# A second Strassen level in four products of a down projection, on one core

## The chip, the core and the metric

The kernel runs on one core of a Trainium2 chip. Its engines are called PE (TensorE: matmuls; PEld: its weight loads), DVE (VectorE), ACT (ScalarE), POOL (GpSimd) and SP (SyncE, which here issues every DMA). A matmul multiplies a stationary 128x128 tile (`lhsT`) with a moving one of up to 512 columns (`rhs`) and adds into PSUM, eight banks of 512 float32 per partition. The metric is the device time of one execution in microseconds; the median of three is given.

## The reference

A pre-norm transformer block over 2048 tokens of width 1024: linear attention, then a gated feed-forward of inner width 3584.

```python
x = A_x
h = x + _A_ref(_layernorm(x), A_wqkv, A_wo)          # linear attention, 32 heads
...
gate = jnp.einsum("bsd,df->bsf", x, W_gate)           # x is here _layernorm(h)
up = jnp.einsum("bsd,df->bsf", x, W_up)
gate = gate * (gate > 0)
h = gate * up
return jnp.einsum("bsf,fd->bsd", h, W_down)           # the down projection
...
h2 = h + _B_ref(_layernorm(h), B_W_gate, B_W_up, B_W_down)
```

## The kernel before

Every large product is done in Strassen's form as Winograd wrote it. A (tokens by inner width) and B are cut in 2 x 2 blocks, and seven products of block sums take the place of eight of blocks. With S1 = A21 + A22, S2 = S1 - A11, S3 = A11 - A21, S4 = A12 - S2 on the left and T1 = B12 - B11, T2 = B22 - T1, T3 = B22 - B12, T4 = B21 - T2 on the right, the products are, numbered as in the code: 1 = A11 B11, 2 = A12 B21, 3 = S4 B22, 4 = A22 T4, 5 = S1 T1, 6 = S2 T2, 7 = S3 T3. Then C11 = 1 + 2, U2 = 1 + 6, U3 = U2 + 7, C12 = U2 + 5 + 3, C21 = U3 + 4, C22 = U3 + 5. Block sums are float16, blocks bfloat16.

**Stages.** Layernorm with the K and V products, Q with attention, the output projection with the second layernorm, the *up stage* (gate and up), the *down stage*. Two halves s = 0, 1 of 512 tokens per block row run through the later stages.

**Up stage.** A loop over `order` runs 28 quads (s, fc): one per half and per block of 128 inner columns (14, fc). A `Quad` is the seven products of one output set in the order 1, 6, 5, 7, 2, 4, 3 on three accumulators: product 1 goes into bank A, and ACT copies it to D (`fork`); 6 is added in A and read out as U2 (`snap`); 5 goes into E; 7 is added in A and read as U3; 2 into D, 4 into A, 3 into E. `Quads.run` moves a quad's last two products behind the next quad's first, so that readers have time. A product is here 8 matmuls of 512 columns. ACT takes the snapshots (`gsnap`), DVE adds, applies the gate and writes the four results `hh` (a11, a12, a21, a22 of the down projection's left side). For s = 0 they stay in memory (`hh0`, 84 KB to 140 KB of each partition), for s = 1 `spill` stores them in `hh_dram`. Gate and up weights come in groups of two blocks (`load_group`), and DVE makes their four right sums (`GW.sums`).

**Down stage.** `down(s)` runs for s = 0 and then 1. Each of the seven products is four token tiles (`tt`) of 14 matmuls of 512 columns, 3 us per tile, and four A banks and four E banks hold a whole product each. DVE makes four left sums of 14 x 512 per half (`sA`, `sB`, `s3`, `s4`) and, for s = 0 only, four right sums `t1` to `t4`, each in two pieces of 7 x 512 (3584 elements), during the products. It adds the residual h, which is loaded again from `h_dram`, and stores the output through the two buffers of `o2_ring`. W_down comes in four loads of 1.8 MB, the first in the up stage; for s = 1 four loads of 1.8 MB bring `hh_dram` back.

```python
        def f6(tt):
            prod(A[tt], tt, sB, t2, False)
            u2[tt] = plus_h(A[tt], 1, tt)
```

**What sets the order.** The whole program is recorded by `Plan.take` as nodes with predecessors; all of them are recorded at line 117, which is why every row of the profile has that line. `order` gives each node a latest start (`late`); `schedule` then simulates the engines with the costs of `cost`, lets each take the ready node with the smallest `late` (TensorE: the smallest place in the program, no more than 6 us of work ahead), counts all DMAs on one serial `wire`, and `issue` writes the instructions out in that order. On the chip each engine runs its own list in order.

Of the kernel before, what the change touches and what calls it, by code (L numbers as in the profile page):

```python
# [9 lines left out]
ALU = mybir.AluOpType  # L10
FP32 = mybir.dt.float32
# [21 lines left out]
class Plan:  # L33
# [75 lines left out]
    def take(self, eng, op, args, k):  # L109
# [31 lines left out]
        for a in outs:  # L141
            name, gs = self.granules(a)
            last, readers = self.state.setdefault(name, ({}, {}))
            for q in gs:
                w = last.get(q)
                if w is not None:
                    v.preds.add(w)
                r = readers.pop(q, None)
                if r:
                    v.preds |= r  # L150
                last[q] = me
# [29 lines left out]
    def schedule(self):  # L181
# [11 lines left out]
        while True:  # L193
# [36 lines left out]
            if v.dma:  # L230
                wire = max(wire, s + v.hold) + v.dma
                end = wire + v.lat - v.dma
# [218 lines left out]
def block_kernel(ctx: ExitStack, tc: tile.TileContext, x, wqkv, wo, wg, wu, wd, out, H: int):  # L451
    nc = tc.nc
# [29 lines left out]
    h_dram = [dram.tile([P, D], BF16, name=f"h_dram{t}") for t in range(ST)]  # L482
    hh_dram = [dram.tile([P, FH, SW], BF16, name=f"hh_dram{q}") for q in range(4)]
# [463 lines left out]
    class Tile_:  # L947
# [54 lines left out]
        def square(self):  # L1002
            h = self.h
            nc.sync.dma_start(out=h_dram[self.t][:], in_=h)
            self.negm = negm = scratch("negm2", 1)
            nc.vector.tensor_scalar(out=negm[:], in0=self.acc[:, 0:1], scalar1=self.acc[:, 1:2], scalar2=-1.0 / D,
                                    op0=ALU.add, op1=ALU.mult)
            self.hn = hn_ring()
            self.ss = scratch("ss", 1)
            tick.late.append(self.square2)  # L1010
# [60 lines left out]
    T_A = (72, 156, 188, 196)  # L1071
    hh1_ring = ring_of([at(180 + i, [SW]) for i in range(8)])

    def hh0(q, fc):
        return at(84 + 4 * fc + q, [SW])

    def gu_quad(s, fc, gw, banks):
# [8 lines left out]
        def dst(q):  # L1086
            return hh0(q, fc) if s == 0 else hh1_ring()

        def spill(q, d):
            if s != 0:  # L1090
                nc.sync.dma_start(out=hh_dram[q][:, fc, :], in_=d)
# [5 lines left out]
        def direct(q):  # L1097
            def f(ps):
# [4 lines left out]
                spill(q, d)  # L1103
# [3 lines left out]
        def added(q):  # L1107
            def f(ps, u):
# [5 lines left out]
                spill(q, d)  # L1114
# [43 lines left out]
    order += [(s, fc) for fc in range(4, FH) for s in range(NS)]  # L1158
    todo = deque([(1, 1, 72), (2, 2, 156), (3, 3, 72), (6, 0, 188), (7, 1, 196)])
    todo.extend((2 * fc, fc, T_A[(fc + 2) % 4]) for fc in range(4, FH))  # L1160
# [12 lines left out]
    b11, b21, b12, b22 = (at(a, [FH, DW]) for a in (164, 0, 14, 28))  # L1173
    t1, t2, t4 = (at(a, [FH, DW], FP16) for a in (42, 56, 178))
    t3 = b12.bitcast(FP16)
    sA, sB = (at(a, [FH, SW], FP16) for a in (70, 150))
    hres_ring = ring_of([at(192 + i, [DW]) for i in range(8)])
    m2_ring = ring_of([at(140 + 2 * i, [DW], FP32) for i in range(4)])
    m3_ring = ring_of([at(a, [DW], FP32) for a in (148, 202)])
    o2_ring = ring_of([at(200 + i, [DW]) for i in range(2)])  # L1180

    def load_wd(b, k, h):
        nc.sync.dma_start(out=b, in_=wd_v[:, k * FH:(k + 1) * FH, h * DW:(h + 1) * DW])

    quads = qs
    for n, (s, fc) in enumerate(order):
# [12 lines left out]
        if n in loads:  # L1199
            load_group(loads[n])  # L1200
        elif n == 24:
            load_wd(b11, 0, 0)
# [5 lines left out]
    load_wd(b21, 1, 0)  # L1208
    load_wd(b12, 0, 1)
    load_wd(b22, 1, 1)  # L1210

    hq = [at(84, [FH, 4, SW])[:, :, q, :] for q in range(4)]
    hf = [at(84, [FH, 4, SW], FP16)[:, :, q, :] for q in range(4)]
    NT = SW // P
    TT = range(NT)
    A = [bank(tt) for tt in TT]
    E = [bank(4 + tt) for tt in TT]

    def vsub(o, a, b, op=ALU.subtract):

        def part(c):
            return lambda: (nc.vector.tensor_tensor(out=o[:, c], in0=a[:, c], in1=b[:, c], op=op), None)[1]

        return [part(slice(g * (FH // 2), (g + 1) * (FH // 2))) for g in range(2)]

    def down(s):
        h11, h12, h21, h22 = hq
        s3, s4 = hf[2], hf[1]
        if s == 1:
            for q in range(4):  # L1230
                nc.sync.dma_start(out=hq[q], in_=hh_dram[q][:, :, :])

        def load_h(q, tt):
            i, j = divmod(q, 2)
            t = (i * HS + s * SW) // P + tt
            y = hres_ring()
            nc.sync.dma_start(out=y, in_=h_dram[t][:, j * DW:(j + 1) * DW])
            return y

        def prod(acc, tt, lhs, rhs, start):  # L1240
            for f in range(FH):
                nc.tensor.matmul(acc, lhsT=lhs[:, f, tt * P:(tt + 1) * P], rhs=rhs[:, f, :],
                                 start=(start and f == 0), stop=(f == FH - 1), skip_group_check=True)

        def plus_h(acc, q, tt):
            m = (m2_ring if q == 1 else m3_ring)()
            nc.vector.tensor_tensor(out=m, in0=acc, in1=load_h(q, tt), op=ALU.add)
            return m

        def store(q, tt, acc, m):  # L1250
            i, j = divmod(q, 2)
            t = (i * HS + s * SW) // P + tt
            o = o2_ring()
            nc.vector.tensor_tensor(out=o, in0=acc, in1=m, op=ALU.add)
            nc.sync.dma_start(out=of[t * P:(t + 1) * P, j * DW:(j + 1) * DW], in_=o)

        def wsum(o, a, b):
            return vsub(o, a, b) if s == 0 else []

        def run(pieces, f):  # L1260

            per = -(-len(pieces) // NT)
            for tt in TT:
                f(tt)
                for p in pieces[tt * per:(tt + 1) * per]:
                    p()

        u2 = {}

        def f1(tt):  # L1270
            prod(A[tt], tt, h11, b11, True)
            nc.scalar.copy(out=E[tt], in_=A[tt])

        def f2(tt):
            prod(E[tt], tt, h12, b21, False)
            store(0, tt, E[tt], load_h(0, tt))

        def f5(tt):
            prod(E[tt], tt, sA, t1, True)

        def f6(tt):
            prod(A[tt], tt, sB, t2, False)
            u2[tt] = plus_h(A[tt], 1, tt)

        def f7(tt):
            prod(A[tt], tt, s3, t3, False)
            store(3, tt, E[tt], plus_h(A[tt], 3, tt))

        def f3(tt):
            prod(E[tt], tt, s4, b22, False)  # L1290
            store(1, tt, E[tt], u2[tt])

        def f4(tt):
            prod(A[tt], tt, h22, t4, False)
            store(2, tt, A[tt], load_h(2, tt))

        run(vsub(sA, h21, h22, ALU.add), f1)
        run(wsum(t1, b12, b11) + vsub(sB, sA, h11), f2)
        run(wsum(t2, b22, t1) + vsub(s3, h11, h21), f5)
        run(wsum(t3, b22, b12) + vsub(s4, h12, sB), f6)  # L1300
        run(wsum(t4, b21, t2), f7)
        run([], f3)
        run([], f4)

    for s in range(NS):
        down(s)
# [51 lines left out]
```

## Time and profile before

| | |
|---|---|
| median of 3 runs | 750.78 us (750.45 to 750.88) |
| the profiled execution | 751.33 us, its span 749.2 us |
| granted TensorE clock | 1.000 of full speed |
| TensorE idle in the span | 14.5 us, of it 0.2 us in the up stage |
| DMA | 78.73 MB, mean 105 GB/s |
| largest DMA groups | `hh_dram` 56 stores of 128 KB; `W_down` 4 loads of 1.8 MB; `hh_dram` 4 loads of 1.8 MB |

The stages by time: the up stage lies from about 235 to 575 us, the down stage behind it to the end. The page's slices of 18.7 us each give the tenths in which an engine was busy (9 is 90% or more) and what the DMA engines moved:

```profile
PE   8899999999999999999999999999999999999998
...
DVE  6987845877987875476446364363438673237132
ACT  5787555656645343333333323233232000010000
...
GB/s 297 124 141 81 130 1 141 1 170 255 166 150 159 128 57 15 154 36 134 28 141 29 42 100 29 138 17 16 113 35 121 238 187 45 239 175 57 26 45 43
```

In a row of instruction groups stand the line, engine, operation, output and input, count, then busy us and mean ns of one, then the idle time of that engine just before and what ended it. Matmul rows overlap: a matmul's row lasts longer than its distance to the next. Engines that are not the bottleneck may idle at no cost.

### The profile page before, as it was taken

Reading aid. Unit: us, or ns where it says so; the run is one execution under the profiler, and the core shown is the slowest. Engines: PE = TensorE matmul, PEld = TensorE weight load, DVE = VectorE, ACT = ScalarE, POOL = GpSimd, SP = SyncE. Lnnn points to the kernel's source line nnn. Section 1 sums busy time; section 2 is a strip of 40 time slices with the busy share of each in tenths; the row PEclk is TensorE's granted clock in tenths of the full one; section 3 lists DMA queues with packets and bytes.
Section 4 is the critical chain, followed back from the end, with each engine's and each line's share of the span. In section 5 each row is a group of like instructions: output and inputs, shape, how many; then the busy total and the mean of one; then the engine's idle time right before and its main releaser. Section 6 shows DMA issues by size and latency. Waiting matters only on the chain.

```text
span 749.2 us, 9354 instructions
## 1 busy us (share of the span) xinstructions
PE 734.7 (98%) x3575; PEld 339.2 (45%) x3575; DVE 447.0 (60%) x677; ACT 268.6 (36%) x526; POOL 45.5 (6%) x62
## 2 busy tenths in 40 slices
PE   8899999999999999999999999999999999999998
PEld 3344545444444444444444444444444444444443
DVE  6987845877987875476446364363438673237132
ACT  5787555656645343333333323233232000010000
POOL 2333000002201110000000000000000000000000
PEclk9999999999999999999999999999999999999999
DMA  9553403079777520514040130400313751751011
GB/s 297 124 141 81 130 1 141 1 170 255 166 150 159 128 57 15 154 36 134 28 141 29 42 100 29 138 17 16 113 35 121 238 187 45 239 175 57 26 45 43
DMA packets 123772, 78.73 MB, mean 105 GB/s; under 512 B 52048, under 2 KB 116560, under 8 KB 123728
## 3 DMA queue, kind: packets, MB, share of 16 engines
q1 hardware_dynamic: 123728, 78.14, 37.4%
q8 instruction: 28, 0.46, 0.3%
q14 instruction: 16, 0.13, 0.0%
HBM read 50.33 MB, written 15.73 MB: 88 GB/s over the span
## 4 chain that ended last, share of the span: by engine, by line
PE 71%; ACT 0%; DVE 0%; issue 0%
PE psum L117 71%; ACT mem L117 0%; DVE mem L117 0%
## 5 line engine op out<-in xcount | busy, mean ns | idle before, releaser
L117 PE MATMUL psum<-mem 128*128 128x512 f16 (+2 forms) x3559 | 733.8, 368 | 9.3 <-DVE mem L117 4.9
L117 PEld LDWEIGHTS <-mem 128*128 128x128 f16 (+1 forms) x3575 | 339.2, 98 | 406.2 <-issue 10.2
L117 DVE TENSOR_TENSOR mem<-psum,mem 128x1024 bf16<-128x1024 f32 (+2 forms) x212 | 169.2, 808 | 234.7 <-PE psum L117 117.5
L117 ACT COPY mem<-psum 128x512 f32<-128x512 f32 (+2 forms) x112 | 85.7, 767 | 188.1 <-PE psum L117 183.5
L117 DVE TENSOR_TENSOR mem<-mem 128x1024 f16<-128x1024 bf16 (+6 forms) x156 | 134.4, 892 | 12.4 <-DMA mem<-h_dram 7.8
L117 ACT COPY psum<-psum 128x512 f32<-128x512 f32 (+1 forms) x62 | 45.7, 737 | 155.2 <-PE psum L117 155.2
L117 ACT ACTIVATE mem<-psum 128x512 bf16<-128x512 f32 x90 | 53.6, 597 | 16.2 <-PE psum L117 15.9
L117 DVE SCALAR_TENSOR_TENSOR mem<-mem 128x512 bf16<-128x512 bf16 (+1 forms) x71 | 58.1, 818 | 1.4
L117 DVE SCALAR_TENSOR_TENSOR mem<-psum,mem 128x512 bf16<-128x512 f32 x66 | 45.5, 689 | 15.2 <-PE psum L117 10.0
L117 POOL TENSOR_SCALAR mem<-mem,tiny 128x1024 bf16<-128x1024 bf16 x30 | 38.9, 1297 | 193.2 <-ACT tiny L117 147.9
L117 ACT ACTIVATE mem<-mem,tiny 128x1024 bf16<-128x1024 bf16 x25 | 28.6, 1144 | 11.7 <-issue 4.7
L117 DVE TENSOR_SCALAR mem<-mem 128x512 bf16<-128x512 bf16 (+1 forms) x49 | 17.9, 367 | 23.7 <-ACT mem L117 23.4
L117 ACT ACTIVATE mem<-mem 128x1024 bf16<-128x1024 f32 (+1 forms) x24 | 25.3, 1056 | 6.3 <-DVE mem L117 5.1
L117 ACT ACTIVATE tiny<-tiny 128x1 f32<-128x1 f32 (+2 forms) x112 | 22.4, 206 | 7.4 <-DVE tiny L117 4.7
L117 DVE TENSOR_TENSOR mem<-psum,tiny 128x384 bf16<-128x384 f32 (+1 forms) x48 | 22.9, 508 | 2.7 <-ACT tiny L117 2.2
L117 ACT ACTIVATE tiny<-psum 128x12 f32<-128x12 f32 (+1 forms) x48 | 8.1, 172 | 17.8 <-PE psum L117 17.8
L117 DVE BATCH_NORM_STATS2 tiny<-mem 128x6 f32<-128x512 bf16 x14 | 9.1, 683 | 5.1 <-DMA mem<-in_A_x_dram 5.1
L117 ACT CAST mem<-psum 128x512 bf16<-128x512 f32 x18 | 10.5, 584 | 2.0 <-PE psum L117 1.6
L117 POOL TENSOR_SCALAR tiny<-tiny 128x1 f32<-128x1 f32 x14 | 5.0, 358 | 32.5 <-ACT tiny L117 14.6
L117 ACT ACTIVATION_READ_ACCUMULATOR mem<-mem,tiny 128x1 f32 x25 | 4.7, 189 | 0.0
L117 DVE TENSOR_SCALAR tiny<-tiny 128x1 f32<-128x1 f32 x16 | 3.4, 211 | 0.4
L117 PE MATMUL psum<-ident,mem 128*128 128x128 bf16 x16 | 1.2, 220 | 1.9 <-DVE mem L117 1.9
(17 smaller groups left out, 12.1 us busy)
## 6 DMA issues: line engine op xcount, KB each, us to landing
mem<-in_A_x_dram SPq DMA_DIRECT2D x32, 256.0 KB, 3.3
mem<-in_B_W_gate_dram SPq DMA_DIRECT2D x14, 512.0 KB, 4.0
mem<-in_B_W_up_dram SPq DMA_DIRECT2D x14, 512.0 KB, 5.2
hh_dram<-mem SPq DMA_DIRECT2D x56, 128.0 KB, 2.0
mem<-in_B_W_down_dram SPq DMA_DIRECT2D x4, 1792.0 KB, 9.8
mem<-hh_dram SPq DMA_DIRECT2D x4, 1792.0 KB, 8.5
mem<-in_A_wqkv_dram SPq DMA_DIRECT2D x12, 512.0 KB, 7.4
h_dram<-mem SPq DMA_DIRECT2D x16, 256.0 KB, 2.4
```

Of the source, the lines that this page charges most:

```text
L117: call = lambda: getattr(getattr(self.nc, eng), op)(*args, **k)
```

## The change

**Order of the products.** The down stage runs product by product, both halves in each, in the order 1, 2, 6, 5, 7, 3, 4. Products 1, 7 and 4 (`shallow`) are as before: 14 matmuls of 512 columns per tile, on three banks.

**Second level.** Products 2, 6, 5 and 3 (`deep`) are cut once more: the left side by half s (rows) and by the first and last seven of the 14 blocks, the right side by seven blocks and by 256 columns. For each of two groups g of two token tiles, a `Quad` runs seven inner products, each 2 tiles x 7 matmuls of 256 columns; both tiles share a bank. `inner_rights` makes four right sums per product, `inner_lefts` four left sums per quad, each 7 x 256 elements, on DVE. Product 1 is kept in float32 in memory (`UM`); products 6, 7 are added to it there, 5 gives `Y`. The snapshots (`usnap`) are adds of PSUM and memory on DVE.

**Up stage.** s = 1 now runs before s = 0. For s = 1, DVE makes S1 to S4 block by block (`spill`) and all seven left operands are stored in `l_dram`; `wd_sums` loads W_down by block, makes T1 to T4 and stores them in `r_dram`. In the down stage each product loads its right side (`right`, r) and its s = 1 left side (`left`, z), 1.8 MB each, into rings of two buffers. For s = 0 the left sums are still made in the down stage (`sums0`).

**Planner.** A matmul that starts a group now claims its whole bank. A DMA is believed to land up to 4 us later, by a quarter of its slack.

```diff
         for a in outs:
             name, gs = self.granules(a)
+            if eng == "tensor" and not accumulates:
+                per = 2048 // self.G
+                gs = [per * b + i for b in sorted({q // per for q in gs}) for i in range(per)]
             last, readers = self.state.setdefault(name, ({}, {}))
             for q in gs:
...
             if v.dma:
                 wire = max(wire, s + v.hold) + v.dma
-                end = wire + v.lat - v.dma
+                end = wire + v.lat - v.dma + min(4000.0, max(0.0, 0.25 * (v.late - s)))
...
-    h_dram = [dram.tile([P, D], BF16, name=f"h_dram{t}") for t in range(ST)]
-    hh_dram = [dram.tile([P, FH, SW], BF16, name=f"hh_dram{q}") for q in range(4)]
+    h_dram = dram.tile([P, ST, D], BF16, name="h_dram")
+    LT = {m: BF16 if m in (1, 2, 4) else FP16 for m in range(1, 8)}
+    l_dram = {m: dram.tile([P, FH, SW], LT[m], name=f"l_dram{m}") for m in range(1, 8)}
+    r_dram = {m: dram.tile([P, FH, D // 2], FP16, name=f"r_dram{m}") for m in (4, 5, 6, 7)}
...
-            nc.sync.dma_start(out=h_dram[self.t][:], in_=h)
+            nc.sync.dma_start(out=h_dram[:, self.t, :], in_=h)
...
-    T_A = (72, 156, 188, 196)
-    hh1_ring = ring_of([at(180 + i, [SW]) for i in range(8)])
+    T_A = (156, 188, 196)
+    hh1 = [at(180 + SH + i, [SW]) for i in range(4)]
+    ss1 = [at(184 + SH + i, [SW], FP16) for i in range(3)]
...
         def dst(q):
-            return hh0(q, fc) if s == 0 else hh1_ring()
-        def spill(q, d):
-            if s != 0:
-                nc.sync.dma_start(out=hh_dram[q][:, fc, :], in_=d)
+            return hh0(q, fc) if s == 0 else hh1[q]
+        def spill():
+            (a11, a12, a21, a22), (s1, s2, s4) = hh1, ss1
+            s3 = a21.bitcast(FP16)
+            for o, x, y, op in ((s1, a21, a22, ALU.add), (s2, s1, a11, ALU.subtract),
+                                (s3, a11, a21, ALU.subtract), (s4, a12, s2, ALU.subtract)):
+                nc.vector.tensor_tensor(out=o, in0=x, in1=y, op=op)
+            for m, f in ((2, a12), (6, s2), (5, s1), (7, s3), (3, s4), (4, a22)):
+                nc.sync.dma_start(out=l_dram[m][:, fc, :], in_=f)
...
-                spill(q, d)
+                if s == 1 and q == 0:
+                    nc.sync.dma_start(out=l_dram[1][:, fc, :], in_=d)
...
-                spill(q, d)
+                if s == 1 and q == 1:
+                    spill()
...
     order = [(0, fc) for fc in range(4)] + [(1, fc) for fc in (2, 3, 0, 1)]
-    order += [(s, fc) for fc in range(4, FH) for s in range(NS)]
+    order += [(s, fc) for fc in range(4, FH) for s in (1, 0)]
     todo = deque([(1, 1, 72), (2, 2, 156), (3, 3, 72), (6, 0, 188), (7, 1, 196)])
-    todo.extend((2 * fc, fc, T_A[(fc + 2) % 4]) for fc in range(4, FH))
+    todo.extend((2 * fc, fc, T_A[(fc - 4) % 3]) for fc in range(4, FH))
...
+    def wd_sums(c):
+        kb = 72 + 6 * (c % 2)
+        (b11, b12), (b21, b22) = [[at(kb + 2 * k + h, [DW]) for h in range(2)] for k in range(2)]
+        t1, t2 = (at(kb + 4 + i, [DW], FP16) for i in range(2))
+        t3, t4 = b12.bitcast(FP16), b21.bitcast(FP16)
+        for k, row in enumerate(((b11, b12), (b21, b22))):
+            nc.sync.dma_start(out=at(kb + 2 * k, [2, DW]),
+                              in_=wd_v[:, k * FH + c, :].rearrange("p (h d) -> p h d", h=2))
+        for o, x, y in ((t1, b12, b11), (t2, b22, t1), (t3, b22, b12), (t4, b21, t2)):
+            nc.vector.tensor_tensor(out=o, in0=x, in1=y, op=ALU.subtract)
+        for m, t in ((5, t1), (6, t2), (7, t3), (4, t4)):
+            nc.sync.dma_start(out=r_dram[m][:, c, :], in_=t)
+    def l1_part(lo, hi):
+        dst = at(72, [12, SW]) if hi == 12 else at(178, [2, SW])
+        nc.sync.dma_start(out=dst, in_=l_dram[1][:, lo:hi, :])
+        return [dst[:, f, :] for f in range(hi - lo)]
...
-        elif n == 24:
-            load_wd(b11, 0, 0)
+        if 8 <= n < 8 + FH:
+            wd_sums(n - 8)
+        if n == 24:
+            r1 = at(164, [FH, DW])
+            load_wd(r1, 0, 0)
+            z1 = l1_part(0, 12)
+        elif n == 26:
+            z1 += l1_part(12, FH)
     quads.flush()
     tick.drain()
-    load_wd(b21, 1, 0)
-    load_wd(b12, 0, 1)
-    load_wd(b22, 1, 1)
...
-    def down(s):
-        h11, h12, h21, h22 = hq
-        s3, s4 = hf[2], hf[1]
-        if s == 1:
-            for q in range(4):
-                nc.sync.dma_start(out=hq[q], in_=hh_dram[q][:, :, :])
...
-        def f3(tt):
-            prod(E[tt], tt, s4, b22, False)
-            store(1, tt, E[tt], u2[tt])
-        def f4(tt):
-            prod(A[tt], tt, h22, t4, False)
-            store(2, tt, A[tt], load_h(2, tt))
-        run(vsub(sA, h21, h22, ALU.add), f1)
-        run(wsum(t1, b12, b11) + vsub(sB, sA, h11), f2)
-        run(wsum(t2, b22, t1) + vsub(s3, h11, h21), f5)
-        run(wsum(t3, b22, b12) + vsub(s4, h12, sB), f6)
-        run(wsum(t4, b21, t2), f7)
-        run([], f3)
-        run([], f4)
-    for s in range(NS):
-        down(s)
+    DEEP = (2, 3, 5, 6)
+    lx = at(0, [FH, SW], FP16)
+    L0 = {1: lq[0], 2: lq[1], 3: lf[1], 4: lq[3], 5: lx, 6: lf[0], 7: lf[2]}
+    z_kb, r_kb = ring_of([14, 28]), ring_of([42, 164])
+    inner_r, inner_l = ring_of([150.5, 178]), [72, 140]
+    h_ring = ring_of([190.5 + i for i in range(3)])
+    o_ring = ring_of([193.5 + i for i in range(2)])
+    m_ring = ring_of([195.5 + 2 * i for i in range(4)])
+    UM = at(56, [NS, 4, DW], FP32)
+    YM = at(84, [FH, 4, DQ], FP32)
+    of_v = of.rearrange("(t p) d -> p t d", p=P)
+    deep_banks = five([bank(b) for b in range(5)])
+    shallow_bank = ring_of([bank(b) for b in (5, 6, 7)])
...
+    def left(m):
+        z = at(z_kb(), [FH, SW], LT[m])
+        nc.sync.dma_start(out=z, in_=l_dram[m][:, :, :])
+        return z
+    def right(m):
+        kb = r_kb()
+        if m in r_dram:
+            r = at(kb, [FH, DW], FP16)
+            nc.sync.dma_start(out=r, in_=r_dram[m][:, :, :])
+        else:
+            r = at(kb, [FH, DW])
+            load_wd(r, int(m != 1), int(m == 3))
+        return r
+    def sums0(o, x, y, op):
+        for g in range(2):
+            c = slice(g * 2 * P, (g + 1) * 2 * P)
+            nc.vector.tensor_tensor(out=o[:, :, c], in0=x[:, :, c], in1=y[:, :, c], op=op)
+    def shallow(m, r, lefts, order, then, seed=None):
+        for s in order:
+            for tt in range(4):
+                b = shallow_bank()
+                if seed is not None:
+                    nc.scalar.copy(out=b, in_=load_h(seed, s, tt, 1, 0, DW)[:, 0, :])
+                for f in range(FH):
+                    if f == FH - 1:
+                        nc.cut()
+                    nc.tensor.matmul(b, lhsT=lefts[s][f][:, tt * P:(tt + 1) * P], rhs=r[:, f, :],
+                                     start=(seed is None and f == 0), stop=(f == FH - 1), skip_group_check=True)
+                then(s, tt, b)
+    def inner_rights(r):
+        y = [[r[:, k * FQ:(k + 1) * FQ, v * DQ:(v + 1) * DQ] for v in range(2)] for k in range(2)]
+        kb = inner_r()
+        t1, t2, t4 = (at(kb + 3.5 * i, [FQ, DQ], FP16) for i in range(3))
+        t3 = y[0][1] if r.dtype == FP16 else None
+        if t3 is None:
+            t3 = y[0][1].bitcast(FP16)
+        for o, a, b in ((t1, y[0][1], y[0][0]), (t2, y[1][1], t1), (t4, y[1][0], t2), (t3, y[1][1], y[0][1])):
+            nc.vector.tensor_tensor(out=o, in0=a, in1=b, op=ALU.subtract)
+        return y[0][0], y[1][0], y[1][1], t4, t1, t2, t3
+    def inner_lefts(x0, x1, g):
+        c = slice(g * 2 * P, (g + 1) * 2 * P)
+        x = [[a[:, u * FQ:(u + 1) * FQ, c] for u in range(2)] for a in (x0, x1)]
+        s1, s2, s4 = (at(inner_l[g] + 3.5 * i, [FQ, 2 * P], FP16) for i in range(3))
+        s3 = x[1][0] if x1.dtype == FP16 else x[1][0].bitcast(FP16)
+        for o, a, b, op in ((s1, x[1][0], x[1][1], ALU.add), (s2, s1, x[0][0], ALU.subtract),
+                            (s4, x[0][1], s2, ALU.subtract), (s3, x[0][0], x[1][0], ALU.subtract)):
+            nc.vector.tensor_tensor(out=o, in0=a, in1=b, op=op)
+        return x[0][0], x[0][1], s4, x[1][1], s1, s2, s3
+    def deep(m, r, x1, src, dst=None, q=None, with_h=None):
+        rights = inner_rights(r)
+        def quad(g):
+            lefts = inner_lefts(L0[m], x1, g)
+            def prod(ps, k, start):
+                for tt in range(2):
+                    for f in range(FQ):
+                        nc.tensor.matmul(ps[:, tt * DQ:(tt + 1) * DQ], lhsT=lefts[k - 1][:, f, tt * P:(tt + 1) * P],
+                                         rhs=rights[k - 1][:, f, :], start=(start and tt == 0 and f == 0),
+                                         stop=(f == FQ - 1), skip_group_check=True)
+            def end(s, v, ps, x):
+                if q is None:
+                    add(dst(s, v, g), pair(ps), x)
+                else:
+                    o = at(o_ring(), [2, DQ])
+                    add(o, pair(ps), x)
+                    store(q, s, 2 * g, v * DQ, DQ, o)
+            def base(s, v):
+                return src(s, v, g) if q is None else with_h(src(s, v, g), q, s, v, g)
+            def usnap(A, which):
+                b = base(which, 1)
+                o = b if q is not None else dst(which, 1, g)
+                add(o, pair(A), b)
+                return o
+            return Quad(prod, fork, usnap, {
+                "c11": lambda D: end(0, 0, D, base(0, 0)), "c21": lambda A: end(1, 0, A, base(1, 0)),
+                "c12": lambda E, u: end(0, 1, E, u), "c22": lambda E, u: end(1, 1, E, u)}, deep_banks)
+        for g in range(2):
+            quads.run(quad(g))
+    def keep(src, q, s, v, g):
+        o = at(m_ring(), [2, DQ], FP32)
+        add(o, src, load_h(q, s, 2 * g, 2, v * DQ, DQ))
+        return o
+    def onto(src, q, s, v, g):
+        add(src, src, load_h(q, s, 2 * g, 2, v * DQ, DQ))
+        return src
+    quads = Quads(lambda: None)
+    shallow(1, r1, ([lq[0][:, f, :] for f in range(FH)], z1), (1, 0),
+            lambda s, tt, b: nc.scalar.copy(out=UM[:, s, tt, :], in_=b))
+    def seven(s, tt, b):
+        add(UM[:, s, tt, :], b, UM[:, s, tt, :])
+        h = load_h(3, s, tt, 1, 0, DW)
+        o = at(o_ring(), [1, DW])
+        for v in range(2):
+            c = slice(v * DQ, (v + 1) * DQ)
+            m = at(m_ring(), [2, DQ], FP32)[:, 0, :]
+            add(m, Y(s, v, tt // 2)[:, tt % 2, :], h[:, 0, c])
+            add(o[:, 0, c], b[:, c], m)
+        store(3, s, tt, 0, DW, o)
+    def step(m, src, dst=None, q=None, with_h=None):
+        r, z = right(m), left(m)
+        if m in DEEP:
+            deep(m, r, z, src, dst, q, with_h)
+            return
+        if quads.prev:
+            quads.flush()
+        def then(s, tt, b):
+            o = at(o_ring(), [1, DW])[:, 0, :] if q is not None else None
+            for v in range(2):
+                c = slice(v * DQ, (v + 1) * DQ)
+                x = src(s, v, tt // 2)[:, tt % 2, :]
+                add(dst(s, v, tt // 2)[:, tt % 2, :] if q is None else o[:, c], b[:, c], x)
+            if q is not None:
+                store(q, s, tt, 0, DW, o.unsqueeze(1))
+        shallow(m, r, [[a[:, f, :] for f in range(FH)] for a in (L0[m], z)], (0, 1),
+                seven if m == 7 else then, q if m != 7 else None)
+    sums0(L0[5], lq[2], lq[3], ALU.add)
+    sums0(L0[7], lq[0], lq[2], ALU.subtract)
+    step(2, U, q=0, with_h=keep)
+    sums0(L0[6], L0[5], lq[0], ALU.subtract)
+    step(6, U, U)
+    sums0(L0[3], lq[1], L0[6], ALU.subtract)
+    step(5, U, Y)
+    step(7, U)
+    step(3, Y, q=1, with_h=onto)
+    step(4, U, q=2, with_h=onto)
+    if quads.prev:
+        quads.flush()
```

`U(s, v, g)` and `Y(s, v, g)` are a quarter's part of those buffers; `load_h` loads h through a ring of three, `store` writes the output; `deep_banks` rotates five banks.

## The prediction

> **What bounds the kernel now.** I read the busy shares first, then the chain of waits, then the stages.
>
> ```profile
> PE 734.7 (98%) x3575; PEld 339.2 (45%) x3575; DVE 447.0 (60%) x677; ACT 268.6 (36%) x526; POOL 45.5 (6%) x62
> ```
>
> ```profile
> 573.01 172.84 PE psum L117 x800
> 745.86 0.03 issue
> 745.88 0.69 DVE mem L117
> ```
>
> TensorE is busy for 98% of the 749.2 us span. The last lines of the chain (start, length, what) show one run of 800 matmuls from 573.01 us to the end without a wait, then one VectorE add and its store. Of these 800, 784 are the down projection (2 halves x 7 products x 4 token tiles x 14), so that stage is tensor time alone: 172.84/800 = 0.216 us per matmul of 512 columns. The end moves only by fewer or shorter matmuls there, or by new waits.
>
> ```profile
> 250.00:573.01 323.01, 322.78 (x1496) 146.25 (x1495) 178.09 (x243) 112.05 (x153) 4.96 (x4) 1.00 0.23 67
> 573.01:745.86 172.85, 172.83 (x800) 78.15 (x799) 78.14 (x74) 5.16 (x9) 0.00 (x0) 1.00 0.40 127
> ```
>
> ```profile
> 37.39:38.32 0.93, 0.93 (x17) 0.93 (x16) 0.93 (x3) 0.73 (x2) 0.00 (x0) 1.00 0.67 159
> ```
>
> The columns are the stretch, its length, busy us and instructions of PE, PEld, DVE, ACT and POOL, granted clock, DMA share, GB/s. Up stage and down stage are full of tensor work at clock 1.00; VectorE has 55% of the first and 45% of the second. The third row is one burst of 16 matmuls of 132 columns, each with its own weight load: 0.93/16 = 58 ns apiece.
>
> **Removed and added on TensorE.** The four products lose 4 x 112 = 448 matmuls of 512 columns. They gain 4 products x 2 groups x 7 inner products x 2 tiles x 7 blocks = 784 of 256 columns, each with a new 128x128 weight tile. No row has 256 columns. Bounds: the straight line through 58 ns at 132 and 216 ns at 512 gives 58 + 124 x 0.416 = 109.6 ns; if the whole cost grew with the columns, twice 58 x 128/132, 112 ns. I take 109.6, because the 58 ns burst shows that even a shorter matmul covers its weight load (98 ns busy each, the next one under way). So 448 x 0.216 = 96.8 us become 784 x 0.1096 = 85.9: **10.9 us less** (9.0 at 112 ns).
>
> Here a rule of the Trainium skill speaks against the change. "TensorE: Matmul & The Clock Gate", section "Back-to-back issue gap", says that in a stream of weight-load and matmul pairs the spacing is about 81 ns at 128 columns and 131 ns at 512. Halfway columns would pay badly: an estimate between those two is 98 ns at 256, so 784 x 98 = 76.8 us would replace 448 x 131 = 58.7 us, 18 us more. The rows here read 58 and 216 ns in just such pairs, so the measurement decides, and narrow matmuls are worth almost their full share.
>
> **VectorE in the down stage.** Durations come from these rows (busy us, mean ns, then idle before), two of the down stage alone and three of the whole span:
>
> ```profile
> L117 DVE TENSOR_TENSOR mem<-mem 128x3584 f16<-128x3584 bf16 x18 | 35.7, 2018 | 9.4 <-DMA mem<-h_dram 7.8 <-DMA mem<-in_B_W_down_dram 1.6
> L117 DVE TENSOR_TENSOR mem<-psum,mem 128x512 bf16<-128x512 f32 x34 | 23.3, 691 | 43.3 <-PE psum L117 32.0 <-DMA out_dram<-mem 10.9 <-issue 0.2
> ```
>
> ```profile
> L117 DVE TENSOR_TENSOR mem<-mem 128x1024 f16<-128x1024 bf16 x70 | 46.2, 692 | 2.3 <-PE psum L117 1.8
> L117 DVE TENSOR_TENSOR mem<-mem 128x512 f16<-128x512 bf16 x36 | 14.8, 426 | 0.0
> L117 DVE TENSOR_TENSOR mem<-psum,tiny 128x256 bf16<-128x256 f32 x16 | 6.7, 421 | 1.0 <-ACT tiny L117 0.6
> ```
>
> The inner operand sums (7 x 256 = 1792 elements) lie between 692 ns at 1024 and 2018 at 3584: 1.09 us on the line, 1.0 back to back; I take 1.05. Adds of 512 out of PSUM are 0.69 alone, 0.60 in a row (a pair took 1.29): 0.65. Sums of 3584 back to back: 1.95.
> Outer sums of half s = 0: 8 x 1.95 = 15.6. Inner right sums 16 and left sums 32: 48 x 1.05 = 50.4. Deep adds out of PSUM, 6 per quad, 8 quads: 48 x 0.65 = 31.2. Adds of h (`keep`, `onto`): 16 x 0.65 = 10.4. Product 7: 8 x (0.65 + 4 x 0.42) = 18.6. Product 4: 16 x 0.42 = 6.7. Sum **133 us** where 78 were. TensorE there needs 336 x 0.216 + 85.9 = 158.5, so VectorE rises from 45% to 84%.
>
> By step, TensorE against VectorE (a step's operands are made in the step before): product 1: 24.2/20.4; 2: 21.4/25.3; 6: 21.4/20.4; 5: 21.4/15.9; 7: 24.2/27.0; 3: 21.4/17.2; 4: 24.2/6.7. Two steps ask for more than TensorE's time, 3.9 and 2.8 us. For the first, product 1 leaves 3.8 us, but `keep` has only four buffers (4 x 0.65 = 2.6 of it can be done early): 1 us is late, and product 6 waits for it. For the second, three shallow banks let the adds trail by up to three tiles (9 us).
>
> **Operands from DRAM.** What I look at (start, length, engine, what; in brackets what the idle time before waited for):
>
> ```profile
> 572.59 7.43 SPq L117 DMA_DIRECT2D mem<-in_B_W_down_dram  x3
> ...
> 586.02 3.96 DVE L117 TENSOR_TENSOR mem<-mem 128x3584 f16<-128x3584 bf16 x2 [1.59 <-DMA mem<-in_B_W_down_dram]
> ...
> 637.09 0.53 SPq L117 DMA_DIRECT2D mem<-hh_dram  x1
> 638.55 2.63 SPq L117 DMA_DIRECT2D out_dram<-mem  x2
> ...
> 646.11 1.29 DVE L117 TENSOR_TENSOR mem<-psum,mem 128x512 bf16<-128x512 f32 x2 [5.29 <-DMA out_dram<-mem]
> ...
> 661.27 0.53 SPq L117 DMA_DIRECT2D mem<-hh_dram  x1
> ...
> 669.78 5.90 DVE L117 TENSOR_TENSOR mem<-mem 128x3584 f16<-128x3584 bf16 x3 [7.82 <-DMA mem<-h_dram]
> ```
>
> The first two lines: two of the 1.8 MB weight loads issued from 572.59 had landed by 586.0 (the sum needs both), 13.4 us for a pair. The last two: one 1.8 MB load took 8.5 us. The middle: a small store issued just behind such a load lands some 7 us later, and VectorE, waiting for its two output buffers, stood 5.29 us, with everything queued behind it on VectorE. TensorE did not notice, because eight banks held 12 us of work.
> Now every step loads a pair (r and z) into buffers freed two steps earlier. With the down stage at 0, product 2 leaves them at 47, the pair for product 5 lands at 60 to 64, and four left sums (4.2) end at 65 to 68, where it starts at 67: on time, or 1 us late. For product 3 they are free at 88.5, landed at 102 to 105, and eight sums (8.4) must join product 7's adds before 112.7. Product 7's own h loads and stores queue behind that pair, and its output ring has two buffers, so VectorE can be held as at 646 us: I take **2 us**, ends 0 and 6. Product 4's seeds on ScalarE wait for h too, but three banks let them run 6 us ahead: nothing (3 us if that cover goes).
>
> **Snapshots.** In a deep quad the sixth product's value is taken out of bank A by VectorE, and the seventh waits to write A; behind it stands all of TensorE. In between lies only the fifth product, 14 x 0.1096 = 1.53 us, against an add of 0.69 and 0.23 for handing over (an estimate: a matmul's row lasts 0.38 against its pace of 0.216, and the chain shows 0.03 from TensorE to VectorE and 0.04 back). That leaves 0.6; an inner sum of 1.05 that stands ahead makes it 0.4 late. The schedule can pull the second product forward. Over 8 quads I take **1 us**, ends 0 and 13.
>
> **Up stage.** Per block, four left sums and four right sums of 512: 14 x 8 x 0.426 = 47.7 us more on VectorE, 178 to 226 of 323 us (70%), hidden under matmuls; without that cover it would be up to 47.7. SP loses 56 stores of hh and one load, gains 98 stores of left operands, 56 of right ones, 28 loads of W_down and three more: some 130 issues x 0.39 = 51 us in 323, and each waiting store holds the weight loads behind it; those are called two quads (24 us) ahead. Bytes: +20 MB, 67 to some 130 GB/s, under the 238 to 297 of the page's fullest slices. New wait: the s = 1 results now have one buffer each, so `c22` of the following quad waits, in quads 4 to 8 where s = 1 comes five times running, for six stores that `spill` issues at the previous `c12`. From that output: 1.2 + 0.7 for it, 1.7 for four sums, 6 x 0.39 issue, 2.2 landing: 8.1 us, and the write comes some 8 us after (four products of 1.73 and an add of 1.22): about even, and four bank pairs cover a slip. I take **0.5 us** for the stage, ends 0 and 4. The planner's two edits (whole banks claimed by a starting matmul, DMAs believed later) issue nothing but can shift any order: 0, ends -1 and 1. The tail has two adds of 256 instead of one of 512: 0.1.
>
> **Sum.** -10.9 + 1 + 2 + 1 + 0.5 + 0.1 = -6.3 us. The profiled execution took 751.33 around its span of 749.2, so it becomes 745.0; the median shown is 0.55 lower: 750.78 - 6.3 = **744.5**.
>
> **Rivals.**
> - *Everything hides* (0.17): the planner finds an order in which loads and sums are always ahead; for it, 84% is not 100%, and up-stage quads with 1.7 us products run with no wait. 750.78 - 10.9 + 0.6 = 740.5.
> - *Operands late* (0.20): small transfers stand behind the pairs at products 2, 5, 7 and 3, at 2 us each instead of the sum's 4 in all: 748.5. For it, 646 and 669 us; against it, 187 GB/s needed (30 MB in 163 us) where slices reach 238.
> - *Snapshots decide, slower* (0.08): two inner sums stand ahead of each sixth-product add and nothing can be pulled forward: 2 x 1.05 + 0.92 - 1.53 = 1.5 us x 8 = 12 in place of 1: 755.5. It decides from about 0.9 us per quad ((6.3 + 1)/8). For it, VectorE at 118% in product 2's step; against it, no more than five of the eight quads are in crowded steps.
> - *Narrow matmuls don't stream* (0.03), as the page's 98 to 131 ns: 18 us slower, 769; the 58 ns burst is against it.
>
> The forecast has 0.52. From no change a measurement here can tell about 0.2%, 1.5 us. Of the late-operand and the snapshot case 0.02 each fall inside that: same 0.04. Slower: 0.06 + 0.03 = 0.09. Faster: 0.87. Range: from just under the hidden case to the late-operand one, 739.8 to 748.6; the slower cases and the rest of late operands are left out.
>
> **What would show it.** Matmuls of 256 columns 109 to 110 ns apart; VectorE some 133 us in the last 163; TensorE idle in the down stage about 4 us, most of it before product 3 with VectorE or a DMA as releaser; up stage still 323 us. I am wrong if 256 columns cost 115 ns or more, if TensorE idles over 9 us, or if the up stage grows by more than 2.

## The result, and the profile after

The changed kernel takes 744.84 us (median of 4 runs, 744.52 to 745.17), the kernel before 750.83 beside it: ratio 0.9919, 95% interval 0.9902 to 0.9936. The forecast was 744.5. The profiled execution has a span of 743.1 us.

Busy us, share and instructions of each engine on the page after:

```profile
PE 722.2 (97%) x3858; PEld 371.7 (50%) x3911; DVE 531.8 (72%) x893; ACT 278.6 (37%) x542; POOL 43.7 (6%) x62
```

VectorE has gained 85 us and TensorE lost 12.5. Some matmul records are missing from a trace, so instructions are counted by their weight loads: 3911 against 3575, the 336 more that the forecast's 784 - 448 says. Stage by stage, with the borders put at the same weight loads in both kernels (number 1000 and 1100 by count, the first of the down stage, the last), before:

```profile
196.30:217.07 20.77, 18.80 (x102) 8.80 (x101) 20.45 (x41) 14.13 (x38) 1.20 (x1) 1.00 0.51 119
217.07:576.25 359.18, 358.94 (x1692) 163.89 (x1691) 204.55 (x297) 127.64 (x207) 9.76 (x8) 1.00 0.29 79
576.25:745.25 169.00, 169.00 (x785) 76.60 (x784) 75.64 (x71) 4.56 (x8) 0.00 (x0) 1.00 0.39 125
745.25:749.20 3.95, 0.59 (x3) 0.10 (x1) 0.69 (x1) 0.00 (x0) 0.00 (x0) 1.00 0.10 33
```

and after:

```profile
196.34:218.25 21.91, 19.04 (x99) 8.78 (x100) 20.44 (x41) 13.13 (x36) 1.59 (x1) 1.00 0.60 145
218.25:579.90 361.65, 357.33 (x1662) 163.59 (x1692) 238.77 (x406) 127.51 (x207) 9.73 (x8) 1.00 0.47 137
579.90:738.91 159.01, 158.10 (x1119) 109.25 (x1119) 128.11 (x178) 13.96 (x24) 0.00 (x0) 1.00 0.54 189
738.91:743.10 4.19, 0.59 (x3) 0.10 (x1) 0.76 (x2) 0.00 (x0) 0.00 (x0) 1.00 0.09 31
```

The first column is the stretch, the second its length, then busy us and counts of PE, PEld, DVE, ACT, POOL, clock, DMA share and GB/s. The down stage became 9.99 us shorter. Three stretches gave part of it back: attention 1.14, the up stage 2.47, the tail 0.24. The sum is -6.1 us, the difference of the spans. From the down stage's start to its end TensorE has one gap, and there is one larger gap 19 us ahead of that stage. TensorE in order of time (start, length, what, count; in brackets the idle time before and who ended it), in two windows:

```profile
552.65 5.78 PE L117 MATMUL psum<-mem 128*128 128x512 bf16 x26
561.12 39.23 PE L117 MATMUL psum<-mem 128*128 128x512 f16 x177 [2.70 <-ACT mem L117]
...
712.11 27.39 PE L117 MATMUL psum<-mem 128*128 128x256 f16 x140 [0.78 <-DVE mem L117]
```

What led to the first of them, on VectorE, ScalarE and SP (an SPq row is an issue of DMAs):

```profile
553.32 1.29 SPq L117 DMA_DIRECT2D mem<-in_B_W_down_dram  x3
...
555.25 0.76 DVE L117 TENSOR_TENSOR mem<-mem 128x512 f16<-128x512 bf16 x2 [2.21 <-DMA mem<-in_B_W_down_dram]
...
557.03 0.42 DVE L117 TENSOR_TENSOR mem<-mem 128x512 f16<-128x512 bf16 x1 [0.42 <-DMA mem<-in_B_W_down_dram]
558.07 0.76 DVE L117 TENSOR_TENSOR mem<-mem 128x512 f16<-128x512 bf16 x2 [0.61 <-DMA mem<-in_B_W_down_dram]
...
560.06 1.01 ACT L117 COPY mem<-psum 128x1024 f32<-128x1024 f32 x1 [6.01 <-DVE mem L117]
```

`wd_sums` is recorded in quads 8 to 21, that is from 335 to 500 us by their place in the program. Yet its loads of W_down run from 467 us, and the last are only issued at 553. VectorE takes its list in order, so it stands for each load (2.21 + 0.42 + 0.61 us). The adds of the running quad queue behind it, then the ScalarE snapshot whose buffer those adds must free, then TensorE. The down stage had been feared, and the stall came at the end of the stage before it.

### The profile page after: what moved, and what is told of

Read it like the earlier page. It is cut to its first block, busy times and chain, and to the rows that moved or that the text cites. A ratio compares the mean times of both kernels' runs of the same rounds, so it can differ in the third digit from the quotient of the medians.

```text
span 743.1 us, 10494 instructions
## 1 busy us (share of the span) xinstructions
PE 722.2 (97%) x3858; PEld 371.7 (50%) x3911; DVE 531.8 (72%) x893; ACT 278.6 (37%) x542; POOL 43.7 (6%) x62
## 4 chain that ended last, share of the span: by engine, by line
PE 64%; DMA 4%; DVE 2%; issue 1%; SPq 1%; ACT 0%; DVEq 0%; ACTq 0%
PE psum L117 64%; DMA mem<-in_B_W_down_dram 2%; DVE mem L117 2%; DMA r_dram<-mem 1%; DMA l_dram<-mem 1%; SPq L117 1%; ACT mem L117 0%; DVEq L1489 0%; DVEq L117 0%; ACTq L117 0%
## 5 line engine op out<-in xcount | busy, mean ns | idle before, releaser
L117 PE MATMUL psum<-mem 128*128 128x512 f16 (+4 forms) x3842 | 721.1, 348 | 16.0 <-DVE mem L117 5.9
L117 PEld LDWEIGHTS <-mem 128*128 128x128 f16 (+1 forms) x3911 | 371.7, 98 | 367.3 <-issue 15.5
L117 DVE TENSOR_TENSOR mem<-psum,mem 128x1024 bf16<-128x1024 f32 (+3 forms) x252 | 185.2, 753 | 143.3 <-ACT mem L117 81.5
L117 DVE TENSOR_TENSOR mem<-mem 128x512 f16<-128x512 bf16 (+8 forms) x332 | 207.4, 663 | 15.4 <-DMA mem<-in_B_W_down_dram 5.2
L117 ACT COPY mem<-psum 128x512 f32<-128x512 f32 (+2 forms) x120 | 90.4, 754 | 209.5 <-PE psum L117 199.7
L117 ACT ACTIVATE mem<-mem 128x1024 bf16<-128x1024 f32 (+1 forms) x24 | 25.3, 1055 | 4.9 <-DVE mem L117 3.8
L117 ACT CAST psum<-mem 128x512 f32<-128x512 bf16 x8 | 4.7, 590 | 24.4 <-DMA mem<-h_dram 13.3
```

The source lines that it names most:

```text
L117: call = lambda: getattr(getattr(self.nc, eng), op)(*args, **k)
```

## The experiments

**Early block loads.** The planner does not release any DMA until 30 us before it is due (`AHEAD`). What `wd_sums` stores is due in the down stage, so its loads and stores wait until then, and two buffers make them a chain. This run releases them at once.

```diff
-            v.left, v.ready = len(v.preds), max(0.0, v.late - self.AHEAD) if v.dma else 0.0
+            v.left, v.ready = len(v.preds), max(0.0, v.late - self.AHEAD) if v.dma and not v.early else 0.0
...
+            nc.early = True
             wd_sums(n - 8)
+            nc.early = False
```

> Theory A: TensorE's 2.9 us stall at 558 us, at the end of the up stage, comes from the W_down block loads, sums and stores that the planner holds back until 30 us before they are due, so that they pile up behind one another in the last 90 us. Freed of that hold they spread over quads 8 to 21, the stall goes, and the time falls by 2 to 3 us, to some 742. Rival B: the stall is the price of 35 us more VectorE work in the up stage, or of the longer list on SP, wherever it lies; then the stall only moves and the time stays within 0.7 us of 744.8. The attention stage keeps its 1.2 us in either case.

Measured: 741.26 us (ratio to the kernel before 0.9878, 0.9862 to 0.9893). TensorE in the last 180 us:

```profile
539.74 168.35 PE L118 MATMUL psum<-mem 128*128 128x512 bf16 x1147
708.87 11.42 PE L118 MATMUL psum<-mem 128*128 128x256 f16 x66 [0.78 <-DVE mem L118]
```

No gap from 540 to 708 us. The last store of right sums is issued at 456 us instead of 562. The up stage takes 358.8 us, less than before the change, with the same VectorE sums in it. TensorE's list is the same as in the changed kernel from end to end; only those of VectorE and SP differ. So Theory A holds: not the work but its place cost 2.9 us. The median fell by 3.6 us; what goes beyond the stage lies ahead of 197 us (last section). The 0.78 near 708 stays.

**The planner's belief in DMAs.** One run takes the later belief away from the changed kernel, one adds it alone to the kernel before.

```diff
-                end = wire + v.lat - v.dma + min(4000.0, max(0.0, 0.25 * (v.late - s)))
+                end = wire + v.lat - v.dma
```

> The planner believes DMAs as before; the rest of the change stays. Theory A: the 1.2 us lost between matmuls 1000 and 1100 (attention, 196 to 217 us) is this edit's, so matmul 1100 starts 1 us or more earlier again; later stages may lose, because loads are then believed on time: total between 743.5 and 750. Rival: the loss belongs to the claimed banks or the other edits, and matmul 1100 still starts at 218.2 us.

> The kernel before with only the planner's later belief in DMAs. Theory A: matmul 1100 starts some 1.2 us later than in the kernel before (218.2 instead of 217.1) and the time rises to about 752. Rival (claimed banks): matmul 1100 stays at 217.1 and the time at 750.8.

Measured: 746.76 us (0.9951, 0.9936 to 0.9965) without it, and 752.33 us (1.0021, 1.0014 to 1.0027) with it alone. Weight loads 1000 to 1100 take 20.77 us before, 21.91 in the changed kernel, 21.05 without the belief, 22.10 in the kernel before with it. The edit costs the attention stage 0.9 to 1.3 us; the claimed banks can hold no more than the 0.3 between 20.77 and 21.05. But without it the end of the up stage is worse:

```profile
534.83 2.98 PE L117 MATMUL psum<-mem 128*128 128x512 f16 x8 [2.60 <-ACT mem L117]
538.03 10.74 PE L117 MATMUL psum<-mem 128*128 128x512 bf16 x47 [0.22 <-issue]
549.76 7.07 PE L117 MATMUL psum<-mem 128*128 128x512 f16 x31 [0.99 <-ACT mem L117]
557.33 2.96 PE L117 MATMUL psum<-mem 128*128 128x512 f16 x13 [0.51 <-DVE mem L117]
```

Four gaps, 4.3 us, where the changed kernel has one of 2.7. Behind the first of them the granted clock also fell to 0.50 for 3.4 us (last section), and the whole up stage takes 365.1 us, 3.4 more than in the changed kernel. The absolute start of matmul 1100 did not tell the theories apart as expected, since all before it wanders (last section); the length of the stretch does.

**Belief only where it helps.** On top of the early loads, the later belief holds only for nodes recorded from the up stage on.

```diff
+                end = wire + v.lat - v.dma + (min(4000.0, max(0.0, 0.25 * (v.late - s))) if v.wary else 0.0)
...
+    nc.wary = True
     for n, (s, fc) in enumerate(order):
```

> On top of the early block loads: the planner's later belief in DMAs holds only for nodes recorded from the up stage on. Theory A: matmuls 1000 to 1100 take 20.8 to 21.1 us again instead of 21.9, and the time falls by some 1 us to 740.3. Rival (the attention stage depends on other edits): no difference, 741.3.

Measured: 739.96 us (0.9853, 0.9838 to 0.9867); the attention stretch takes 20.76 us. As Theory A says.

**Six buffers for h.** In the changed kernel, the gap before 712 us has this in front of it on SP, VectorE and ScalarE:

```profile
694.22 0.42 SPq L117 DMA_DIRECT2D mem<-r_dram  x1
694.68 0.45 SPq L117 DMA_DIRECT2D mem<-l_dram  x1
695.41 1.97 SPq L117 DMA_DIRECT2D mem<-h_dram  x2
...
707.44 0.69 DVE L117 TENSOR_TENSOR mem<-mem 128x512 f32<-128x512 f32 x1 [1.56 <-DMA mem<-h_dram]
...
711.37 0.69 DVE L117 TENSOR_TENSOR mem<-psum,mem 128x512 f32<-128x512 f32 x1 [0.61 <-PE psum L117]
711.85 0.59 ACT L117 CAST psum<-mem 128x512 f32<-128x512 bf16 x1 [9.04 <-DMA mem<-h_dram]
```

Two small h loads are issued right behind the operand pair of product 4. The one that VectorE waits for at 707.44 us took 11.9 us; the median h load takes 2.4.

```diff
-    h_ring = ring_of([190.5 + i for i in range(3)])
+    h_ring = ring_of([190.5, 191.5, 192.5, 161, 162, 163])
```

> On top of the early block loads: six instead of three buffers for h. TensorE's only stall in the down stage (0.95 us, near the end of product 3, waiting for a snapshot on VectorE) follows 1.6 us in which VectorE waits for an h load that lies behind the operand pair. Theory A (the late h load makes the snapshot late): loads are issued earlier, the stall falls under 0.3 us, time some 0.5 to 1 us under that of the early block loads alone (741.3). Rival (the snapshot is late because VectorE has too much to do there): the stall and the time stay.

Measured: 739.43 us (0.9858, 0.9837 to 0.988), and TensorE to the end:

```profile
539.73 194.16 PE L118 MATMUL psum<-mem 128*128 128x512 f16 x1280
```

One row without a gap. The down stage takes 158.17 us instead of 159.01 or 159.02. The load that VectorE stood for is now one of two issued from 685.2 us on, ahead of the pair (688.4 and 692.5), and no engine waits for an h load. The stall was a late h load, not too much work.

The late load worked by a detour. VectorE had caught up before the gap: it waits 0.61 us for TensorE before the add at 711.37. In the schedule the inner products 5 and 2 of that quad were drawn ahead while the add after inner product 6 waited for h. So nothing was left to put behind inner product 7 while its snapshot was taken, and ScalarE's seed for product 4, late for want of h as well, came only at 711.85. The count agrees: behind the gap lie 140 matmuls, 28 of the last two inner products and 112 of product 4.

The time fell by 1.8 us, more than the 0.85 that the stage shows; the rest lies ahead of 197 us (last section).

**Left sums twice.** How much room has VectorE?

```diff
-        for o, a, b, op in ((s1, x[1][0], x[1][1], ALU.add), (s2, s1, x[0][0], ALU.subtract),
-                            (s4, x[0][1], s2, ALU.subtract), (s3, x[0][0], x[1][0], ALU.subtract)):
+        for o, a, b, op in ((s1, x[1][0], x[1][1], ALU.add), (s2, s1, x[0][0], ALU.subtract),
+                            (s1, x[1][0], x[1][1], ALU.add), (s2, s1, x[0][0], ALU.subtract),
+                            (s4, x[0][1], s2, ALU.subtract), (s4, x[0][1], s2, ALU.subtract),
+                            (s3, x[0][0], x[1][0], ALU.subtract)):
```

> Three of the four inner left sums of every quad are made twice over, 24 more VectorE instructions of about 1.05 us, 25 us in all; results unchanged, matmuls unchanged. It asks how much room VectorE had in the down stage (128 us busy of 159). Theory A (VectorE is close to the bound in the steps of products 2, 6 and 5, as the sums by step say): the stage grows by 10 to 16 us, the time to 755 to 761, with TensorE waiting for VectorE between 604 and 668 us. Rival (the sums run far ahead and VectorE has ample room): under 3 us more.

Measured: 763.34 us (1.0157, 1.0135 to 1.0179). The down stage grew from 159.0 to 178.0 us, and VectorE's busy time in it from 128.1 to 152.0: 19 us for 23.8 us of work. That is more than Theory A's 16, and far from its rival. Some 1.7 of the 19 us (an estimate, half of 3.41) are a granted clock of 0.50 from 699.2 to 702.6 us in this execution (last section). The stretch of products 2, 6 and 5 by the changed kernel's times:

```profile
604.00:668.40 64.40, 55.03 (x493) 48.09 (x492) 63.64 (x71) 3.44 (x6) 0.00 (x0) 1.00 0.46 170
```

VectorE is busy 63.64 of 64.40 us, and TensorE is the one that waits. So the changed kernel's schedule took up 5 to 7 us of added work in the whole stage (23.8 less 19, or less 17.3 without the clock).

**Three deep products.** `DEEP = (2, 5, 6)`, product 3 at one level.

> The change with product 3 back at one level (112 matmuls of 512 columns for 196 of 256); products 2, 6 and 5 stay deep. Theory A (the gain is TensorE's alone, 2.8 us per deep product at 109 ns per narrow matmul): the down stage takes 159.0 + 2.8 = 161.8 us, less the 0.95 us snapshot stall that lay in product 3: 160.9 to 161.8; time 746.7 to 747.6. Rival (VectorE's load takes back part of what each deep product gives, as it did for the fifth): the down stage grows by under 1.4 us.

Measured: 746.62 us (0.9944, 0.9928 to 0.996); down stage 160.86 us, at the lower edge of Theory A, with no gap in it (the stall lay in product 3). By matmuls a deep product is worth 2.8 us, of which product 3 kept 1.85; the rest is its stall.

**Five deep products.** `DEEP = (2, 3, 4, 5, 6)`, once on the changed kernel, once with all three repairs (early loads, belief from the up stage on, six h buffers), and beside it the three repairs with four.

> Product 4 goes through the second level too: 112 matmuls of 512 columns become 196 of 256, 24.2 - 21.4 = 2.8 us less on TensorE, while VectorE gets some 18 us more in the last step. Theory A (TensorE bounds the down stage, VectorE at 80% hides): 1 to 3 us faster, 742 to 744. Rival (VectorE bounds it in crowded steps): products 3 and 4 now crowd one after the other and the time is 745 or more.

> Early block loads, later belief only from the up stage on, six buffers for h, and product 4 through the second level too. If the parts add up: 744.8 - 3 - 1 - 0.7 - 1.2 (what five deep products gave) to -2.8 (what the matmuls alone give) = 737.3 to 739. Rival (VectorE is full in the last two steps): 740 or more.

> Early block loads, later belief only from the up stage on, six buffers for h, and four deep products as in the change. Theory A (the three repairs are independent stalls of TensorE and add up): attention 20.8 us, up stage 358.8, down stage 158.2, tail as in the change: 744.8 - 3 - 1.1 - 0.8 = 739.9 by stages, and by the two runs that had two of the three repairs 738.3 to 739; below every run so far. Rival (they share one cause, so one repair takes the other's gain): 739.4 or more. If it is also under the run with five deep products (740.9), the fifth product costs more at the end than its matmuls save.

Measured: five on the changed kernel 743.58 us (0.9909, 0.9896 to 0.9921), inside Theory A's range; five with the repairs 740.85 (0.9866, 0.9851 to 0.988); four with the repairs **739.13** (0.9845, 0.9831 to 0.9858). The last lies between its two theories (738.3 to 739 and 739.4). It is the lowest here, by 0.3 us over six h buffers without the attention repair, which the runs don't separate: medians cannot show that all three repairs add up, while the stages do (20.75, 358.79 and 158.10 us). Five deep products shorten the repaired down stage by only 0.7 us, to 157.4, and then lengthen the end: from the last weight load to the end of the span 6.3 us against 4.2. So the sum of the second expectation (737.3 to 739) missed, and its rival's 740 or more came, though only in part for the rival's reason: TensorE waits 1.2 us for VectorE in the stage, and 2.1 us are lost behind it. The end with five:

```profile
731.41 1.69 PE L119 MATMUL psum<-mem 128*128 128x256 f16 x14 [0.24 <-DVE mem L119]
...
732.75 1.29 DVE L119 TENSOR_TENSOR mem<-psum,mem 128x512 bf16<-128x512 f32 x2 [0.20 <-DMA out_dram<-mem]
735.41 0.69 DVE L119 TENSOR_TENSOR mem<-psum,mem 128x512 bf16<-128x512 f32 x1 [1.37 <-DMA out_dram<-mem]
```

The last adds wait for the two output buffers, which a product of 1.5 us fills faster than a store empties them; with one level a tile takes 3 us. This is read from the trace; more output buffers were not tried.

## Why the prediction was right

The size was right by luck, because two errors met: the down stage kept 3 us that had been granted to its stalls (-9.99 against -6.9), and 3 us were lost before it (3.6 in the up stage and attention against 0.5). The matmul term was right; the terms for stalls were not, and by its own sign, an up stage longer by more than 2 us, the prediction's account of that stage is wrong.

- **Narrow matmuls, -10.9.** Right. In a stretch of the changed kernel with nothing but 256 columns there are 196 weight loads in 21.40 us, 109.2 ns apiece (forecast 109.6). The rule of "TensorE: Matmul & The Clock Gate" in the Trainium skill, section "Back-to-back issue gap" (131 ns at 512 columns, by estimate 98 at 256), which made the change 18 us slower, does not hold here. The down stage shrank by 9.99 us with a gap of 0.9 in it.

```profile
604.20:625.60 21.40, 21.40 (x198) 19.08 (x196) 19.15 (x23) 2.29 (x4) 0.00 (x0) 1.00 0.41 136
```

- **VectorE, 133 us.** 128.1 measured; the inner sums read 1083 ns (1.05 in a row was taken). What the steps' table got wrong is where the work lies: it had 25.3 us for product 2's step and 27.0 for product 7's, against TensorE's 21.4 and 24.2; the trace, cut at the same times, has 19.2 and 20.1, and 23.7 in the step of product 1, since whatever was ready was made early (likewise 20.1 in product 5's step, where the table had 15.9). So the 1 us for a late product 6 did not come. That the sum is near the edge was right: 23.8 us more cost 19.
- **Operand pairs, 2 us.** The times were right: the pair for product 5 is issued at 625.9 and 627.4 us (46.0 and 47.5 after the stage's start; 47 was reckoned) and the pair for product 3 at 667.3 and 668.9 (87.4 and 89.0; 88.5). The cost was not: no engine waits for a pair in this stage. VectorE waits for h loads, 1.6 us, and for output buffers, 1.4; ScalarE waits 13.3 us for h loads. What the term feared, small loads caught behind a pair, came a step later than reckoned, behind the pair for product 4, and cost 0.85 us in product 3 and not ahead of it. That the h load came late for want of a free buffer is shown by the six buffers; that it then stood behind the pair, by its 11.9 us against 2.4. No run tries the two apart. Product 4's seeds, put at nothing, were late too and could not fill the gap.
- **Snapshots, 1 us.** The one gap is a snapshot's, 0.8 to 0.9 us in place of 1, once in 8 quads, but not the snapshot that was priced: it follows inner product 7 and not 6. Its cause was the h load, so this and the last term were one. The slower rival, at 0.08, did not come; the doubled sums show what it would have looked like. TensorE's idle time in the stage was 0.9 us and not about 4.
- **Up stage, 0.5.** Too small: 2.5. The step that failed is "hidden under matmuls": work was counted over 323 us as if it were spread there, and I did not ask when the planner would release it, though `AHEAD` and the due time in the down stage stood in the code. With the loads early, it is hidden entirely.
- **Planner's edits, 0 with ends -1 and 1.** 1.14 in attention, just outside its end, most of it the later belief's. In the profiled executions that belief buys 3.4 us at the end of the up stage (some 1.7 of it the clock's, by estimate), as long as the block loads are late.
- **Tail, 0.1.** 0.24.
- **Rivals.** "Everything hides" (740.5) is what the repaired kernels reach: 739.1 to 740. "Operands late" did not come.

## What to carry to other kernels

A matmul half as wide costs half as long here even with a fresh weight tile each (109 against 216 ns), so a Strassen level is worth its eighth as long as VectorE can make the sums; reckon that by step, and expect the order to level it. Work that is moved into a stage with idle engines is only hidden if something also releases it early: look at what its due time, its buffers and the planner's hold make of its start. When a sum of small terms comes out right, compare it stage by stage: here stalls whose repair brought 4.9 us (1.16 in attention, 2.86 in the up stage, 0.91 in the down stage) stood behind a total that was 0.3 us off.

## What the hardware showed that was not expected

The start of an execution is not repeatable to a microsecond. The 1000th weight load starts between 194.4 and 197.8 us over the twelve profiled executions. The changed kernel, early block loads, six buffers for h and left sums twice have the same list on every engine up to there, and it starts at 196.3, 195.9, 194.4 and 196.2 us.

Part of it is the granted clock, the third number from the end of each row. In the changed kernel:

```profile
24.50:27.91 3.41, 1.34 (x7) 0.60 (x7) 3.34 (x7) 1.60 (x6) 0.21 (x1) 1.00 0.01 3
27.91:31.32 3.41, 3.19 (x8) 1.17 (x8) 2.22 (x5) 2.64 (x6) 1.43 (x2) 0.50 0.09 18
```

with the left sums made twice:

```profile
23.37:26.78 3.41, 0.60 (x4) 0.14 (x3) 3.34 (x6) 1.68 (x5) 0.57 (x1) 1.00 0.00 0
26.78:30.19 3.41, 3.19 (x9) 1.20 (x9) 3.23 (x7) 1.95 (x5) 1.10 (x1) 0.50 0.00 0
```

and with early block loads:

```profile
23.68:27.09 3.41, 2.03 (x10) 0.71 (x8) 3.34 (x4) 3.03 (x7) 0.00 (x0) 1.00 0.36 130
27.09:30.50 3.41, 2.66 (x12) 1.29 (x14) 3.38 (x8) 1.64 (x4) 1.00 (x2) 1.00 0.00 0
```

In the first two the clock falls to 0.50 for 3.41 us; in the third it does not. The twelve traces show a common step of 3.413 us: between the first change of the clock and the last, each stretch at 1.00 or 0.50 is a whole number of such steps (7, 1 and 209 in the changed kernel). Where the steps begin differs from one execution to the next. The clock fell in seven places ahead of the last 10 us, each time after a step in which TensorE was busy for about 18% to 47% of it (39% and 18% in the rows above; 60% in the third, without a fall). The least busy step without a fall behind it had about 42%. So a gap may cost twice or once, depending on how the steps cut it: the 2.6 us gap without the later belief left a step at 24% and brought a fall, the 2.7 us gap of the changed kernel left one at 42% and brought none.

Five of the twelve executions have a fall near 28 us and reach the 1000th load at 196.2 to 197.8 us; the other seven reach it at 194.4 to 196.3. All four runs of the changed kernel have a mean clock of 0.998, as one fall gives, while three of the four with early block loads have 1.000, so their medians differ by more than the stages do.

The Trainium skill ("TensorE: Matmul & The Clock Gate", section "What's actually happening") says that an idle window drops the clock to half and that the window which decides is free-running. The half and the shifting steps agree with the traces; but the steps that brought a fall here were not idle. So differences of a microsecond between kernels that share their beginning are best read stage by stage.
